# Mish part of a fused attention and MLP kernel: token tiles of 512 columns in place of 384

## The chip, the cores and the metric

The kernel runs on one core of a Trainium2 chip. The metric is the device time of one execution, in microseconds (us). The profile counts the core's span from the first to the last instruction, and names the engines: PE is TensorE's matmul stream and PEld its weight loads, DVE is VectorE, ACT is ScalarE, POOL is GpSimd, SP is SyncE, which issues the transfers.

## The reference, cut to what matters

Three layers follow each other: a landmark attention (4 batches of 576 tokens, 8 heads of 64), a gated MLP, and a Mish MLP. The change lies in the last one alone. Its input x has 2304 tokens (4 times 576) by 512.

```python
def _moe2_ref(x, w_in, w_out):          # 2304 x 512, 512 x 2048, 2048 x 512
    h = x @ w_in
    sp = np.where(h > 20.0, h, np.log1p(np.exp(np.minimum(h, 20.0))))
    g = h * np.tanh(sp)
    return (g @ w_out).astype(np.float32)
```

## The kernel before

Attention and the gated MLP are issued as steps in an order that a table (`ORDER`, line 24) writes out; each step is for one engine and each engine works its steps in that order. At its end the step list leaves `Y[b]` (512 features by 576 tokens for each batch, in SBUF). Behind it stands the Mish part, lines 1047 to 1131, as plain loops. Only the part behind the table, and the four steps `yh`/`yl` of the table that split the first tile's activations (`add_ys`, line 1029), depend on the tile width `TT`.

Every product of the Mish part keeps fp32 accuracy by splitting both operands in a high part (`fp32r`) and the rest: `mm3` (line 188) makes three matmuls, high times high (L189), high times rest (L190), rest times high (L191). Each of them has its own weight load of 128 by 128.

The part works on 6 tiles of `TT` = 384 tokens, and in each on 16 blocks `f` of 128 hidden features: 96 iterations `n`. One call `p2(n)` (line 1107) issues for one iteration:

- `z_mm(n)`, the first product: 4 blocks `k` of 128 input features, `mm3` each, so 12 matmuls. The stationary operand is a block of w_in, the moving one the split activations `ys(t, k, hl)`, 384 columns wide. The result is bank `n % 4` of PSUM (`bank[0:4]`, printed as ps_83 to ps_86).
- `o_mm(n - 3)`, the second product of the iteration three before: for each of the tile's 3 blocks `c` of 128 tokens one `mm3`, so 9 matmuls. Stationary are the split Mish values `gb(n, hl)`, moving is a block of w_out, 512 columns wide. They add up over the 16 blocks `f` in one accumulator bank per `c`, and three of the four banks `bank[4:8]` (ps_87 to ps_90) are in use in a tile; the next tile starts one bank further (`(3 * t + c) % 4`). After the last `f`, ACT (c = 0, 2) and DVE (c = 1) copy the accumulators to `osb`, and SP issues a store for each.
- `tick(n)` (line 1101): ACT takes Mish of the bank twice, into `emx` in fp32 (L1103) and into `gb(n, 0)` in fp32r (L1104); DVE subtracts the two into `gb(n, 1)` (L1105). Both `gb` and `emx` have three places, used in turn (`n % 3`).
- for `n` under 12, the remaining weights: one block of w_in or w_out is split by ACT and POOL, and a later one is loaded by SP and decoded by DVE and ACT.
- `split_y` for the next tile, on ACT (high part) and DVE (rest), one `k` in each of four iterations.

Since `z_mm(n)` stands ahead of `o_mm(n - 3)` on PE, ACT and DVE have the stretch of some two iterations to bring `gb(n)`, before PE wants it. In the first three iterations there is no second product, and in the last three calls no first one. `gb(n, 0)` may only be written when `o_mm(n - 3)` has read the same place.

Of the kernel before, what the change touches and what calls it, by code (L numbers as in the profile page):

```python
# [7 lines left out]
F32 = mybir.dt.float32  # L8
F32R = mybir.dt.float32r
# [3 lines left out]
ACTF = mybir.ActivationFunctionType  # L13
# [138 lines left out]
def kernel(  # L152
# [14 lines left out]
    nc = tc.nc  # L167
    V, G, S, T = nc.vector, nc.gpsimd, nc.scalar, nc.tensor
    B, S_LEN = v.shape[0], v.shape[1]
# [1 line left out]
    NP = H // 2  # L171
    BLK_T = S_LEN // L
    HALF = S_LEN // 2
    TT = 384
    NS = w1.shape[1] // 128
    scale = 1.0 / float(D) ** 0.5

    def f32(ap):
        return ap.bitcast(F32)
# [8 lines left out]
    def mm3(o, lh, ll, rh, rl, first, last):  # L188
        T.matmul(out=o, lhsT=lh, rhs=rh, start=first, stop=False)  # L189
        T.matmul(out=o, lhsT=lh, rhs=rl, start=False, stop=False)  # L190
        T.matmul(out=o, lhsT=ll, rhs=rh, start=False, stop=last)  # L191
# [5 lines left out]
    def top_bits(e, w):  # L197
        q = w.bitcast(U16)
        if e == "ACT":

            S.activation(w[..., 0], q[..., 1], ACTF.Copy, scale=2.0 ** -13, bias=2.0 ** -14 - 0.5)  # L201
        else:
            V.tensor_scalar(q[..., 0], q[..., 1], 13, None, op0=ALU.logical_shift_right)

    def sign(w):
        q = w.bitcast(U16)
        V.tensor_scalar(q[..., 1], q[..., 3], 0x8000, None, op0=ALU.bitwise_and)  # L207

    def rescale(w):
        S.activation(f32(w[..., 1]), f32(w[..., 1]), ACTF.Copy, scale=2.0 ** -112)  # L210
# [5 lines left out]
    def copy(e, o, x):  # L216
        if e == "ACT":
            S.activation(o, x, ACTF.Copy)  # L218
        else:
            (G if e == "POOL" else V).tensor_scalar(o, x, 1.0, 0.0, op0=ALU.mult, op1=ALU.add)  # L220

    def less(e, o, x, hi):
        (G if e == "POOL" else V).tensor_tensor(o, x, f32(hi), op=ALU.subtract)
# [6 lines left out]
    def kept(tag, shape, dtype, name):  # L230

        return pe.tile(shape, dtype, tag=tag, name=name)
# [4 lines left out]
    Y = {}  # L237
# [10 lines left out]
    RAW = kept("RAW", [128, 4, 512, 2], I32, "raw")  # L248
    LATE = {}
    bank = [ps.tile([128, 512], F32, name=f"ps{i}") for i in range(8)]  # L250
# [12 lines left out]
    def step(name, eng, after, fn, take=(), free=()):  # L263
        for key in free:
            users.setdefault(key, set()).add(name)
        steps[name] = ((eng,) if isinstance(eng, str) else eng,
                       [a for a in dict.fromkeys(after) if a in steps], fn, dict(take), tuple(free))
# [6 lines left out]
    def got(key):  # L274
        pool, i = at[key]
        return pools[pool][i]
# [620 lines left out]
    HS = []  # L897

    def swap(e):
        attn_pool.close()  # L900
        pw = ctx.enter_context(tc.tile_pool(name="pw", bufs=1, reuse_waits="tile"))
        HS.extend(pw.tile([128, 8 * 2 * HALF], F32R, name=f"hs{i}") for i in range(2))
        HS.append(pw.tile([128, 4, 1024], F32R, name="wx"))
        HS.append(pw.tile([128, TT], F32R, name="gx"))
        HS.append(pw.tile([128, 3, TT], F32, name="emx"))

    def hs(u):
        return HS[got(f"hs {u}")].rearrange("p (k h s) -> p k h s", k=8, h=2)
# [29 lines left out]
    NF = wi2.shape[1] // 512  # L938
    wq = [(k, j, i) for j in range(NF) for k in (0, 1) for i in range(4)]

    def late(tag, shape, dtype, name):
        if name not in LATE:
            LATE[name] = kept(tag, shape, dtype, name)
        return LATE[name]

    def wpart(n, i):

        if n < 4:
            x = HS[2][:, n]
        elif n < 7:  # L950
            x = M[n - 4]
        elif n < 11:
            x = late(f"W{(n - 7) // 2}", [128, 2, 1024], F32R, f"wxw{(n - 7) // 2}")[:, (n - 7) % 2]
        elif n == 11:
            x = late("A", [128, 1024], F32R, "wxa")
        elif n < 20:
            x = late(f"H{(n - 12) // 2}", [128, 2, 1024], F32R, f"wx{(n - 12) // 2}")[:, n % 2]
        elif n < 28:
            x = W3[(n - 20) // 4][:, 2 * (n % 4):2 * (n % 4) + 2].rearrange("p a n -> p (a n)")
        else:  # L960
            x = HS[got("hs 7")][:, (n - 28) * 1024:(n - 27) * 1024]
        return x[:, i * 512:(i + 1) * 512]
# [7 lines left out]
    def w_load(n, r):  # L970
        k, j, i = wq[n]
        src = wi2[i * 128:(i + 1) * 128, j * 512:(j + 1) * 512] if k == 0 else wo2[(4 * j + i) * 128:(4 * j + i + 1) * 128, :]
        nc.sync.dma_start(out=r, in_=words(src))

    def w_raw(n):
        n = EARLY + (n - EARLY) % RAW6 if n >= EARLY else n
        if n >= EARLY + 4:
            return late("LT", [128, 2, 512, 2], I32, "wl")[:, n - EARLY - 4]
        return got(f"x{n}")
# [46 lines left out]
    def ys0(k, hl):  # L1026
        return HS[got("ys")][:, (2 * k + hl) * TT:(2 * k + hl + 1) * TT]

    def add_ys(k):
        step(f"yh {k}", "ACT", ["sh 7 0", f"ye 0 {k}", f"ye 1 {k}"] + [f"yh {i}" for i in range(k)],  # L1030
             lambda e: copy(e, ys0(k, 0), Y[0][:, k, 0:TT]), {} if k else {"ys": "hs"})
        step(f"yl {k}", "DVE", [f"yh {k}"], lambda e: less(e, ys0(k, 1), Y[0][:, k, 0:TT], ys0(k, 0)))

# [11 lines left out]


    NT = out.shape[0]
    NTILE = NT // TT
    E = HS[4]
    R = HS[got("ys")].rearrange("p (r s) -> p r s", r=12)  # L1050
    GX = [HS[3], HS[got("hs 7")][:, 4096:4096 + TT]]

    def ys(t, k, hl):
        return (late("RAW", [128, 8, TT], F32R, "ys") if t % 2 else R)[:, 2 * k + hl, :]

    def split_y(t, k):
        done = 0
        while done < TT:
            b, s = divmod(t * TT + done, S_LEN)
            w = min(TT - done, S_LEN - s)  # L1060
            o = slice(done, done + w)
            copy("ACT", ys(t, k, 0)[:, o], Y[b][:, k, s:s + w])
            less("DVE", ys(t, k, 1)[:, o], Y[b][:, k, s:s + w], ys(t, k, 0)[:, o])
            done += w

    def gb(n, hl):
        return GX[hl] if n % 3 == 2 else R[:, 8 + 2 * (n % 3) + hl, :]

    NFC = 4 * NF
    NN = NTILE * NFC  # L1070
    zt, ot, oc = {}, {}, [0]

    def z_mm(n):
        t, f = divmod(n, NFC)
        c = slice((f % 4) * 128, (f % 4 + 1) * 128)
        p = zt[n] = bank[n % 4][:, 0:TT]
        for k in range(4):
            u = 8 * (f // 4) + k
            mm3(p, wpart(u, 0)[:, c], wpart(u, 1)[:, c], ys(t, k, 0), ys(t, k, 1), k == 0, k == 3)

    def o_mm(n):
        t, f = divmod(n, NFC)
        u = 8 * (f // 4) + 4 + f % 4
        for c in range(3):
            if f == 0:
                ot[c] = bank[4 + (3 * t + c) % 4]
            s = slice(c * 128, (c + 1) * 128)
            mm3(ot[c], gb(n, 0)[:, s], gb(n, 1)[:, s], wpart(u, 0), wpart(u, 1), f == 0, f == NFC - 1)
        if f == NFC - 1:
            osb = late("LT", [128, 4, 512], F32, "osb")  # L1090
            for c in range(3):
                o = osb[:, oc[0] % 4]
                oc[0] += 1
                if c % 2 == 0:
                    S.activation(o, ot[c], ACTF.Copy)
                else:
                    V.tensor_copy(o, ot[c])
                r0 = t * TT + c * 128
                nc.sync.dma_start(out=out[r0:r0 + 128, :], in_=o)

    def tick(n):
        x = E[:, n % 3, :]
        S.activation(x, zt[n], ACTF.Mish)  # L1103
        S.activation(gb(n, 0), zt.pop(n), ACTF.Mish)  # L1104
        V.tensor_tensor(gb(n, 1), x, f32(gb(n, 0)), op=ALU.subtract)  # L1105

    def p2(n):
        if n < NN:
            z_mm(n)
        if n >= 3:  # L1110
            o_mm(n - 3)
        if n < NN:
            tick(n)
        u = EARLY + n
        if u < len(wq):
            copy("ACT", wpart(u, 0), f32(w_raw(u)[..., 0]))
            less("POOL", wpart(u, 1), f32(w_raw(u)[..., 0]), wpart(u, 0))
            if u + RAW6 < len(wq):
                w_load(u + RAW6, w_raw(u))
            if n >= 2 and u - 2 + RAW6 < len(wq):  # L1120
                r = w_raw(u - 2 + RAW6)
                top_bits("DVE", r)
                sign(r)
                rescale(r)
                join(r)
        split_at = (12, 13, 14, 15) if n < NFC else (4, 7, 10, 13)
        if n % NFC in split_at and n + NFC < NN:
            split_y(n // NFC + 1, split_at.index(n % NFC))

    for n in range(NN + 3):  # L1130
        p2(n)


# [38 lines left out]
```

## Time and profile before

| | us |
|---|---|
| median of 3 runs (lowest to highest) | 787.62 (783.45 to 1238.11) |
| the profiled execution's own time | 785.8 |
| its span | 784.0 |
| PE busy in the span | 758.1 |
| ACT busy / DVE busy in the span | 343.7 / 348.6 |
| first matmul of the Mish part starts at | 378.19 |
| last matmul of the Mish part starts at | 779.74 |

The times of the rows are counted from the span's start; the profiled execution's own time has 1.8 us more than its span. A matmul's row gives its start and how long it was under way; matmuls overlap, so the pace of PE is read from the distance of two starts, here called a step. The duration of a row is longer than a step.

### The profile page before, as it was taken

How to read it: one execution, taken by the hardware profiler on the slowest of the kernel's cores; microseconds unless marked ns; L12 is line 12 of the kernel's file. 1: busy time of each engine (PE TensorE's matmuls, PEld its weight loads, DVE VectorE, ACT ScalarE, POOL GpSimd, SP SyncE). 2: the span in 40 equal slices, each digit the busy share in tenths (PEclk: the TensorE clock that was granted, in tenths of full speed). 3: DMA queues.
4: the chain of work that ended last, by engine and by line, in shares of the span. 5: the costliest groups of instructions: out<-in, count | busy, mean ns of one | idle time of the engine just before them, and what ended most of it. 6: DMA issues, size and time to landing. Idle time of an engine off the chain costs nothing.

```text
span 784.0 us, 13585 instructions
## 1 busy us (share of the span) xinstructions
PE 758.1 (97%) x5380; PEld 650.6 (83%) x5380; DVE 348.6 (44%) x719; ACT 343.7 (44%) x772; POOL 119.2 (15%) x120
## 2 busy tenths in 40 slices
PE   6887999999999999999999999999999999999998
PEld 2644457888799889999998998999999999899896
DVE  5878867887875663755271221121111112111111
ACT  5456465666653664876444222232222222222221
POOL 0427100520153213331232000000000000000000
PEclk8989899999999999999999999999999999999999
DMA  8993255742431314343220010010010001001001
GB/s 311 376 320 97 82 188 161 253 129 82 135 109 56 107 55 135 109 135 108 81 82 0 1 41 1 0 41 1 1 40 2 1 1 41 0 1 41 1 0 41
DMA packets 38384, 65.96 MB, mean 84 GB/s; under 512 B 3888, under 2 KB 20400, under 8 KB 38320
## 3 DMA queue, kind: packets, MB, share of 16 engines
q1 hardware_dynamic: 38320, 65.09, 24.9%
q8 instruction: 42, 0.69, 0.4%
q14 instruction: 22, 0.18, 0.1%
HBM read 60.36 MB, written 4.72 MB: 83 GB/s over the span
## 4 chain that ended last, share of the span: by engine, by line
PE 90%; DVE 5%; DMA 2%; issue 1%; ACT 1%; SPq 1%; POOL 0%; DVEq 0%; ACTq 0%; POOLq 0%
PE ps L189 26%; PE ps L191 26%; PE ps L190 25%; PE ps L356 6%; PE ps L850 2%; DVE raw L207 2%; PE ps L450 2%; DMA raw<-in_wo_dram 1%; DVE raw L214 1%; DMA raw<-in_w_dram 1%; PE ps L528 1%; PE ps L646 1%; PE ps L587 1%; PE ps L566 0%; PE ps L506 0%
## 5 line engine op out<-in xcount | busy, mean ns | idle before, releaser
L1105 DVE TENSOR_TENSOR hs<-emx,hs 128x384 fp32r<-128x384 f32 x64 | 35.7, 559 | 202.1 <-ACT hs L1104 201.9
L1103 ACT ACTIVATE emx<-ps 128x384 f32<-128x384 f32 x96 | 47.1, 490 | 130.3 <-PE ps L191 130.3
L189 PE MATMUL ps<-hs,W 128*128 128x288 f32 (+1 forms) x304 | 91.8, 302 | 0.0
L190 PE MATMUL ps<-hs,W 128*128 128x288 f32 (+1 forms) x304 | 91.4, 301 | 0.0
L191 PE MATMUL ps<-hs,W 128*128 128x288 f32 (+1 forms) x304 | 91.4, 301 | 0.0
L207 DVE TENSOR_SCALAR raw<-raw 128x512 uint16<-128x512 uint16 x84 | 72.7, 894 | 37.7 <-ACT raw L201 37.3
L189 PE MATMUL ps<-AT,M 128*128 128x288 f32 x256 | 78.2, 305 | 0.1
L191 PE MATMUL ps<-AT,M 128*128 128x288 f32 x256 | 75.5, 295 | 0.0
L190 PE MATMUL ps<-AT,M 128*128 128x288 f32 x256 | 75.5, 295 | 0.0
L356 PE MATMUL ps<-wo,raw 128*128 128x512 f32 x128 | 62.9, 651 | 7.2 <-DVE raw L214 7.2
L210 ACT ACTIVATE raw<-raw 128x512 f32<-128x512 f32 x84 | 55.8, 678 | 28.7 <-DVE raw L207 24.6
L201 ACT ACTIVATE raw<-raw 128x512 int32<-128x512 uint16 x79 | 52.6, 672 | 29.1 <-DMA raw<-in_w_dram 14.3
L1104 ACT ACTIVATE hs<-ps 128x384 fp32r<-128x384 f32 x64 | 31.5, 492 | 76.0 <-PE ps L190 76.0
L1105 DVE TENSOR_TENSOR hs<-emx,gx 128x384 fp32r<-128x384 f32 x32 | 17.9, 558 | 99.9 <-ACT gx L1104 99.7
L356 PEld LDWEIGHTS ps<-wo,raw 128*128 128x128 f32 x128 | 27.0, 215 | 40.3 <-issue 29.1
L190 PEld LDWEIGHTS ps<-hs,W 128*128 128x128 f32 x304 | 57.4, 189 | 0.5
L189 PEld LDWEIGHTS ps<-hs,W 128*128 128x128 f32 x304 | 57.0, 187 | 1.0 <-ACT y L218 0.4
L191 PEld LDWEIGHTS ps<-hs,W 128*128 128x128 f32 x304 | 57.3, 189 | 0.0
L189 PEld LDWEIGHTS ps<-AT,M 128*128 128x128 f32 x256 | 48.0, 188 | 7.2 <-issue 2.1
L191 PEld LDWEIGHTS ps<-AT,M 128*128 128x128 f32 x256 | 48.1, 188 | 0.0
L190 PEld LDWEIGHTS ps<-AT,M 128*128 128x128 f32 x256 | 48.1, 188 | 0.0
L218 ACT ACTIVATE a<-ps 128x288 f32<-128x288 f32 x64 | 26.1, 410 | 36.0 <-PE ps L191 35.6
(217 smaller groups left out, 1712.9 us busy)
## 6 DMA issues: line engine op xcount, KB each, us to landing
raw<-in_w_dram SPq DMA_DIRECT2D x128, 128.0 KB, 2.6
raw<-in_wo_dram SPq DMA_DIRECT2D x22, 512.0 KB, 4.6
raw<-in_w3T_dram SPq DMA_DIRECT2D x32, 256.0 KB, 6.9
raw<-in_wi_dram SPq DMA_DIRECT2D x14, 512.0 KB, 4.2
k<-in_kT_dram SPq DMA_DIRECT2D x8, 576.0 KB, 8.1
q<-in_qT_dram SPq DMA_DIRECT2D x8, 576.0 KB, 8.6
out_dram<-osb SPq DMA_DIRECT2D x18, 256.0 KB, 2.1
vt<-in_v_dram SPq DMA_DIRECT2D x4, 1024.0 KB, 8.3
```

Source lines behind the costliest of these rows:

```text
L189: T.matmul(out=o, lhsT=lh, rhs=rh, start=first, stop=False)
L190: T.matmul(out=o, lhsT=lh, rhs=rl, start=False, stop=False)
L191: T.matmul(out=o, lhsT=ll, rhs=rh, start=False, stop=last)
L201: S.activation(w[..., 0], q[..., 1], ACTF.Copy, scale=2.0 ** -13, bias=2.0 ** -14 - 0.5)
L207: V.tensor_scalar(q[..., 1], q[..., 3], 0x8000, None, op0=ALU.bitwise_and)
L210: S.activation(f32(w[..., 1]), f32(w[..., 1]), ACTF.Copy, scale=2.0 ** -112)
L218: S.activation(o, x, ACTF.Copy)
L356: T.matmul(out=got(f"acc{i}"), lhsT=f32(got(f"w3{n}")[:, o:o + 128, 0]), rhs=WO0[j // 4][:, j % 4], start=j == 0, stop=j == 7)
L450: T.matmul(out=sc[0:w, i, p * 64:p * 64 + 64], lhsT=st["q"][:, p, t0:t0 + w], rhs=bdk[:, p, :], start=True, stop=True)
L1103: S.activation(x, zt[n], ACTF.Mish)
L1104: S.activation(gb(n, 0), zt.pop(n), ACTF.Mish)
L1105: V.tensor_tensor(gb(n, 1), x, f32(gb(n, 0)), op=ALU.subtract)
```

## The change

The tile width becomes 512, and the tiles are listed with their width, four of 512 tokens and a last one of 256. So there are 80 iterations. In a tile of 512, `z_mm` has 12 matmuls of 512 columns and `o_mm` 12 (four blocks `c`); in the last tile 12 of 256 columns and 6. The second product follows two iterations behind (`o_mm(n - 2)`), `gb` has two places and `emx` one. The accumulators are `bank[4 + c]` in each tile, and the copies out go to ACT for even `c` and to DVE for odd `c`.

```diff
-    TT = 384
+    TT = 512
...
-        HS.append(pw.tile([128, TT], F32R, name="gx"))
-        HS.append(pw.tile([128, 3, TT], F32, name="emx"))
+        HS.append(pw.tile([128, 2, TT], F32R, name="gx"))
+        HS.append(pw.tile([128, TT], F32, name="emx"))
...
-    NTILE = NT // TT
+    tiles = [(t0, min(TT, NT - t0)) for t0 in range(0, NT, TT)]
     E = HS[4]
-    R = HS[got("ys")].rearrange("p (r s) -> p r s", r=12)
-    GX = [HS[3], HS[got("hs 7")][:, 4096:4096 + TT]]
+    R = HS[got("ys")][:, 0:8 * TT].rearrange("p (r s) -> p r s", r=8)
+    GX = [HS[3][:, 0], HS[3][:, 1], HS[got("ys")][:, 8 * TT:9 * TT], HS[got("hs 7")][:, 4096:4096 + TT]]
...
     def gb(n, hl):
-        return GX[hl] if n % 3 == 2 else R[:, 8 + 2 * (n % 3) + hl, :]
+        return GX[2 * (n % 2) + hl][:, 0:tiles[n // NFC][1]]
...
-        p = zt[n] = bank[n % 4][:, 0:TT]
+        p = zt[n] = bank[n % 4][:, 0:tiles[t][1]]
...
-        for c in range(3):
-            if f == 0:
-                ot[c] = bank[4 + (3 * t + c) % 4]
+        for c in range(w // 128):
             s = slice(c * 128, (c + 1) * 128)
-            mm3(ot[c], gb(n, 0)[:, s], gb(n, 1)[:, s], wpart(u, 0), wpart(u, 1), f == 0, f == NFC - 1)
+            mm3(bank[4 + c], gb(n, 0)[:, s], gb(n, 1)[:, s], wpart(u, 0), wpart(u, 1), f == 0, f == NFC - 1)
...
-        x = E[:, n % 3, :]
+        x = E[:, 0:tiles[n // NFC][1]]
...
-        if n >= 3:
-            o_mm(n - 3)
+        if n >= 2:
+            o_mm(n - 2)
...
-    for n in range(NN + 3):
+    for n in range(NN + 2):
```

`split_y` cuts a tile where a batch ends, as before, but by the tile's own width: the pieces of the second tile are 64 and 448 columns in place of 192 and 192.

On PE, at the first second product, the order before is this (M_1032 is a block of w_out, wx and wxw are blocks of w_in, hs_2358 holds the split activations and before also `gb`):

```order
L189 MATMUL ps_88<-M_1032,hs_2358 128x512
L190 MATMUL ps_88<-M_1032,hs_2358 128x512
L191 MATMUL ps_88<-M_1032,hs_2358 128x512
L189 MATMUL ps_89<-M_1032,hs_2358 128x512
L190 MATMUL ps_89<-M_1032,hs_2358 128x512
L191 MATMUL ps_89<-M_1032,hs_2358 128x512
L189 MATMUL ps_83<-hs_2358,wxw_3263 128x384
L190 MATMUL ps_83<-hs_2358,wxw_3263 128x384
L191 MATMUL ps_83<-hs_2358,wxw_3263 128x384
```

and of the changed kernel:

```order
L189 MATMUL ps_88<-M_1032,gx 128x512
L190 MATMUL ps_88<-M_1032,gx 128x512
L191 MATMUL ps_88<-M_1032,gx 128x512
L189 MATMUL ps_89<-M_1032,gx 128x512
L190 MATMUL ps_89<-M_1032,gx 128x512
L191 MATMUL ps_89<-M_1032,gx 128x512
L189 MATMUL ps_90<-M_1032,gx 128x512
L190 MATMUL ps_90<-M_1032,gx 128x512
L191 MATMUL ps_90<-M_1032,gx 128x512
L189 MATMUL ps_86<-hs_2358,wx 128x512
L190 MATMUL ps_86<-hs_2358,wx 128x512
```

Three accumulators with a 384-wide first product behind them become four with a 512-wide one, and the width of the moving operand no longer changes between the two products.

On PE, in the last tile, before (the last matmuls of the first product with the last block of w_in, and the second product behind it):

```order
L189 MATMUL ps_86<-ys,W_66 128x384
L190 MATMUL ps_86<-ys,W_66 128x384
L191 MATMUL ps_86<-ys,W_66 128x384
L189 MATMUL ps_90<-hs_2359,gx 128x512
L190 MATMUL ps_90<-hs_2359,gx 128x512
L191 MATMUL ps_90<-hs_2359 128x512
L189 MATMUL ps_87<-hs_2359,gx 128x512
L190 MATMUL ps_87<-hs_2359,gx 128x512
L191 MATMUL ps_87<-hs_2359 128x512
L189 MATMUL ps_88<-hs_2359,gx 128x512
L190 MATMUL ps_88<-hs_2359,gx 128x512
L191 MATMUL ps_88<-hs_2359 128x512
```

and now:

```order
L189 MATMUL ps_86<-hs_2358,W_66 128x256
L190 MATMUL ps_86<-hs_2358,W_66 128x256
L191 MATMUL ps_86<-hs_2358,W_66 128x256
L189 MATMUL ps_87<-hs_2359,hs_2358 128x512
L190 MATMUL ps_87<-hs_2359,hs_2358 128x512
L191 MATMUL ps_87<-hs_2359 128x512
L189 MATMUL ps_88<-hs_2359,hs_2358 128x512
L190 MATMUL ps_88<-hs_2359,hs_2358 128x512
L191 MATMUL ps_88<-hs_2359 128x512
L189 MATMUL ps_87<-hs_2359,gx 128x512
```

The first product is 256 wide there, and one second product has six matmuls in place of nine.

On DVE, where the first tile's accumulators are copied out, before:

```order
L223 TENSOR_TENSOR ys<-y_2581,ys 128x192
L223 TENSOR_TENSOR ys<-y_3391,ys 128x192
L1105 TENSOR_TENSOR hs_2358<-emx,hs_2358 128x384
L1105 TENSOR_TENSOR hs_2359<-emx,gx 128x384
L1097 COPY osb<-ps_88 128x512
L1105 TENSOR_TENSOR hs_2358<-emx,hs_2358 128x384 x2
L1105 TENSOR_TENSOR hs_2359<-emx,gx 128x384
```

and now:

```order
L223 TENSOR_TENSOR ys<-y_2581,ys 128x64
L223 TENSOR_TENSOR ys<-y_3391,ys 128x448
L1103 TENSOR_TENSOR gx<-emx,gx 128x512
L1096 COPY osb<-ps_88 128x512
L1096 COPY osb<-ps_90 128x512
L1103 TENSOR_TENSOR hs_2359<-emx,hs_2358 128x512
L1103 TENSOR_TENSOR gx<-emx,gx 128x512
```

DVE has two accumulators to copy in place of one at the end of a wide tile, and the subtraction of the next Mish values stands behind both.

## Rows read from the trace of the kernel before

**Rows 1.** The page: busy time by engine, the TensorE clock by slice, the chain by engine.
```profile
PE 758.1 (97%) x5380; PEld 650.6 (83%) x5380; DVE 348.6 (44%) x719; ACT 343.7 (44%) x772; POOL 119.2 (15%) x120
...
PEclk8989899999999999999999999999999999999999
...
PE 90%; DVE 5%; DMA 2%; issue 1%; ACT 1%; SPq 1%; POOL 0%; DVEq 0%; ACTq 0%; POOLq 0%
```

**Rows 2.** Windows: length; busy us (x) of PE, PEld, DVE, ACT, POOL; clock, DMA, GB/s.
```profile
378.19:779.97 401.78, 401.78 (x2018) 363.93 (x2016) 84.41 (x148) 119.62 (x251) 17.29 (x12) 1.00 0.05 18
391.12:730.29 339.17, 339.17 (x1702) 307.26 (x1702) 73.10 (x129) 100.41 (x214) 13.20 (x9) 1.00 0.05 17
```

**Rows 3.** Timeline of PE in the steady state: start us, us, engine line op.
```profile
499.64 0.39 PE L189 MATMUL ps<-W,hs 128*128 128x512 f32 x1
...
501.72 0.33 PE L189 MATMUL ps<-ys,W 128*128 128x384 f32 x1
...
503.82 0.39 PE L189 MATMUL ps<-hs,hs 128*128 128x512 f32 x1
```

**Rows 4.** Timeline of PE from the product before through the start of the Mish part.
```profile
375.02 0.30 PE L189 MATMUL ps<-hs,W 128*128 128x288 f32 x1
...
378.19 0.34 PE L189 MATMUL ps<-hs,wx 128*128 128x384 f32 x1
...
380.30 0.33 PE L189 MATMUL ps<-hs,wx 128*128 128x384 f32 x1
...
386.54 0.39 PE L189 MATMUL ps<-M,hs 128*128 128x512 f32 x1
```

**Rows 5.** Timeline of PE in the last second products.
```profile
773.85 0.39 PE L189 MATMUL ps<-hs,hs 128*128 128x512 f32 x1
...
777.93 0.39 PE L189 MATMUL ps<-hs,gx 128*128 128x512 f32 x1
...
779.74 0.39 PE L191 MATMUL ps<-hs 128*128 128x512 f32 x1
```

**Rows 6.** Groups by form from 360 us: busy, mean ns, idle before.
```profile
L1103 ACT ACTIVATE emx<-ps 128x384 f32<-128x384 f32 x96 | 47.1, 490 | 130.3 <-PE ps L191 130.3
...
L1105 DVE TENSOR_TENSOR hs<-emx,hs 128x384 fp32r<-128x384 f32 x64 | 35.7, 559 | 202.1 <-ACT hs L1104 201.9
...
L1095 ACT ACTIVATE osb<-ps 128x512 f32<-128x512 f32 x12 | 7.2, 599 | 21.5 <-PE ps L191 21.5
...
L1097 DVE COPY osb<-ps 128x512 f32<-128x512 f32 x6 | 4.2, 692 | 17.5 <-PE ps L191 17.5
...
L223 DVE TENSOR_TENSOR ys<-y,ys 128x192 fp32r<-128x192 f32 x8 | 2.5, 351 | 0.0
...
L189 PEld LDWEIGHTS ps<-hs,W 128*128 128x128 f32 x46 | 8.6, 187 | 0.0
```

**Rows 7.** Timeline of ACT and DVE in the same iteration as rows 3.
```profile
501.75 0.49 ACT L1104 ACTIVATE hs<-ps 128x384 fp32r<-128x384 f32 x1 [1.42 <-PE ps L190]
...
502.27 0.56 DVE L1105 TENSOR_TENSOR hs<-emx,hs 128x384 fp32r<-128x384 f32 x1 [3.16 <-ACT hs L1104]
```

**Rows 8.** Timeline of DVE in the first iterations.
```profile
390.39 0.56 DVE L1105 TENSOR_TENSOR hs<-emx,hs 128x384 fp32r<-128x384 f32 x1
...
394.73 0.56 DVE L1105 TENSOR_TENSOR hs<-emx,hs 128x384 fp32r<-128x384 f32 x1
```

**Rows 9.** Timeline at the first change of tile: DVE, then PE.
```profile
439.89 0.62 DVE L223 TENSOR_TENSOR ys<-y,ys 128x192 fp32r<-128x192 f32 x2
...
440.62 0.38 PE L190 MATMUL ps<-ys,wx 128*128 128x384 f32 x1
...
440.85 0.34 PE L191 MATMUL ps<-ys,wx 128*128 128x384 f32 x1
```

**Rows 10.** Timeline of ACT: first split of activations, and the last copy out.
```profile
363.39 1.75 ACT L218 ACTIVATE hs<-y 128x384 fp32r<-128x384 f32 x4
...
780.17 0.60 ACT L1095 ACTIVATE osb<-ps 128x512 f32<-128x512 f32 x1 [0.76 <-PE ps L191]
```

More of the change, by code (lines that the diff above doesn't have):

```diff
@@ L1047 @@
     NT = out.shape[0]
-    NTILE = NT // TT
+    tiles = [(t0, min(TT, NT - t0)) for t0 in range(0, NT, TT)]
     E = HS[4]
-    R = HS[got("ys")].rearrange("p (r s) -> p r s", r=12)
-    GX = [HS[3], HS[got("hs 7")][:, 4096:4096 + TT]]
+    R = HS[got("ys")][:, 0:8 * TT].rearrange("p (r s) -> p r s", r=8)
+    GX = [HS[3][:, 0], HS[3][:, 1], HS[got("ys")][:, 8 * TT:9 * TT], HS[got("hs 7")][:, 4096:4096 + TT]]
     def ys(t, k, hl):
-        return (late("RAW", [128, 8, TT], F32R, "ys") if t % 2 else R)[:, 2 * k + hl, :]
+        return (late("RAW", [128, 8, TT], F32R, "ys") if t % 2 else R)[:, 2 * k + hl, 0:tiles[t][1]]
     def split_y(t, k):
+        t0, w = tiles[t]
         done = 0
[L1058 to L1064, printed above, removed]
+        while done < w:
+            b, s = divmod(t0 + done, S_LEN)
+            n = min(w - done, S_LEN - s)
+            o = slice(done, done + n)
+            copy("ACT", ys(t, k, 0)[:, o], Y[b][:, k, s:s + n])
+            less("DVE", ys(t, k, 1)[:, o], Y[b][:, k, s:s + n], ys(t, k, 0)[:, o])
+            done += n
+    NFC = 4 * NF
+    NN = len(tiles) * NFC
+    zt, ot, oc = {}, {}, [0]
     def gb(n, hl):
-        return GX[hl] if n % 3 == 2 else R[:, 8 + 2 * (n % 3) + hl, :]
-    NFC = 4 * NF
-    NN = NTILE * NFC
-    zt, ot, oc = {}, {}, [0]
+        return GX[2 * (n % 2) + hl][:, 0:tiles[n // NFC][1]]
     def z_mm(n):
@@ L1082, in o_mm @@
         t, f = divmod(n, NFC)
+        t0, w = tiles[t]
         u = 8 * (f // 4) + 4 + f % 4
-        for c in range(3):
-            if f == 0:
-                ot[c] = bank[4 + (3 * t + c) % 4]
+        for c in range(w // 128):
             s = slice(c * 128, (c + 1) * 128)
-            mm3(ot[c], gb(n, 0)[:, s], gb(n, 1)[:, s], wpart(u, 0), wpart(u, 1), f == 0, f == NFC - 1)
+            mm3(bank[4 + c], gb(n, 0)[:, s], gb(n, 1)[:, s], wpart(u, 0), wpart(u, 1), f == 0, f == NFC - 1)
         if f == NFC - 1:
             osb = late("LT", [128, 4, 512], F32, "osb")
-            for c in range(3):
-                o = osb[:, oc[0] % 4]
-                oc[0] += 1
+            for c in range(w // 128):
+                o = osb[:, c]
                 if c % 2 == 0:
-                    S.activation(o, ot[c], ACTF.Copy)
+                    S.activation(o, bank[4 + c], ACTF.Copy)
                 else:
-                    V.tensor_copy(o, ot[c])
-                r0 = t * TT + c * 128
-                nc.sync.dma_start(out=out[r0:r0 + 128, :], in_=o)
+                    V.tensor_copy(o, bank[4 + c])
+                nc.sync.dma_start(out=out[t0 + c * 128:t0 + (c + 1) * 128, :], in_=o)
     def tick(n):
-        x = E[:, n % 3, :]
+        x = E[:, 0:tiles[n // NFC][1]]
         S.activation(x, zt[n], ACTF.Mish)
```

## The prediction

> **What bounds the kernel now.** I read the page first. PE is busy in 97% of the span, its clock is at the full level of 2.4 GHz in nearly every slice, and 90% of the chain that ended last is PE's [rows 1]. Then the windows: the Mish part is 401.78 us, half of the span, and PE is busy in all of it at the full clock, while DVE has 84 us and ACT 120 us of work [rows 2]. So only what changes PE's own pace, or makes PE wait, can move the time. The pace comes from the timeline. In the steady state nine matmuls of the second product take 501.72 - 499.64 = 2.08 us, a step of 231.2 ns, and twelve of the first take 503.82 - 501.72 = 2.10 us, 175.3 ns [rows 3]. The window from 391.12 to 730.29 holds 1702 matmuls, so 81 iterations of 21 in 339.17 us, 4.187 us each [rows 2]: the pattern of rows 3 repeats without a gap.
>
> Two places show a faster step. The first products of iterations 1 to 3, which stand behind one another with no second product between them, take (386.54 - 380.30)/36 = 173.3 ns a step; that of iteration 0, behind 288-wide matmuls, took 2.11 us for twelve, 175.8 ns [rows 4]. The 18 matmuls of the second product that follow one another at the end take (777.93 - 773.85)/18 = 226.7 ns [rows 5]. So where the width of the moving operand stays the same the step is shorter, and where it has just changed it is longer: 0.026 us a first product and 0.041 us a second one. ACT and DVE work during the fast stretches too, so their traffic is not the likely reason. The 288-wide product before has (378.19 - 375.02)/24 = 132.1 ns [rows 4]. From 132.1 over 173.3 to 226.7 the step grows by 0.42 to 0.43 ns a column; what is left over at zero columns, some 10 to 13 ns, is paid for every matmul whatever its width.
>
> **The change part by part.** The columns streamed stay the same, 96 x (12 x 384 + 9 x 512) = 884,736 before and after. The number of matmuls falls from 2016 to 64 x 24 + 16 x 18 = 1824: the first product has 192 fewer, the second still 864.
>
> The sum for PE, by the steps without a change of width for the four wide tiles, where every moving operand is now 512 wide: 64 x 24 x 226.7 ns = 348.2 us. In the last tile the widths alternate (256 and 512), so I take the longer second-product step: 16 x 6 x 231.2 ns = 22.2 us. A 256-wide step is not in the trace. The line from 288 and 384 gives 118 ns, that from 384 and 512 gives 120; I take 119.5, and as bounds 115.5 (173.3 x 256/384) and 132.1, the row next to it. 192 x 119.5 = 22.9 us, and 16 x 0.026 = 0.4 us for the changes of width. Together 393.7 us against 401.8, so **8.1 us less**. The other end for the 512-wide step is the 231.2 ns that the second product has now [rows 3]: then the wide tiles take 355.1 us and the gain is 1.2 us. I take 226.7 because the same pattern, the same operands and the same engine gave it as soon as the widths stopped changing.
>
> On the weight loads a record and a rule differ. A load is recorded with 187 ns, and this while the 288-wide steps were 132 ns [rows 4, 6], so the records overlap and do not set the pace there. The Trainium skill ("TensorE: Matmul & The Clock Gate", LDWEIGHTS) has a load of 128 columns at P / 1.2, about 107 ns. By that rule the 256-wide step of 119.5 ns still covers the load, and the 22.9 us stay; if a load really held the array for the recorded time they would be 36.1 us. No row here shows a mean step under 130 ns with such loads, so the point is open; it is the third rival.
>
> Work off PE. A Mish of 384 columns is 490 ns; of 512 I take the 600 ns of ACT's 512-wide copy, and at most 490 x 512/384 = 653. A subtraction is 559 ns; from the 351 ns at 192 columns, 1.04 ns a column, 512 come to 0.69 us, as DVE's 512-wide copy has it; at most 745 [rows 6]. ACT and DVE keep two thirds of their time free [rows 2], so the amounts cost nothing under PE's steps.
>
> The shorter pipeline. Today ACT's second Mish waits until the second product that reads the old place is nearly through; it starts 0.03 us after the next first product does, and the subtraction follows 0.52 us later [rows 3, 7]. Afterwards the same wait exists: after `z_mm(n)` comes `o_mm(n - 2)`, 12 x 226.7 = 2.7 us, then Mish 0.6 and the subtraction 0.7, so `gb(n)` is there about 4.1 us behind the end of `z_mm(n)`. PE wants it after four products, 10.9 us. Slack 6.8 us; in the last tile 1.39 + 0.03 + 0.9 = 2.3 us against 5.6. Behind the waiting Mish on ACT stand only splits for the next tile and weights. The single `emx`: the next Mish may start when the subtraction is over, 4.1 us against a period of 5.4, so nothing is late. If this cover were gone, each wait would stand on PE; the second rival from below prices one.
>
> The first iterations: DVE, with decoding and the waits on ACT, needs 394.73 - 390.39 = 4.34 us an iteration [rows 8], slightly more than PE's 4.19, and lags. With 0.13 us more for the subtraction (0.19 at most) it is about 4.5 us against PE's 5.44, so the lag shrinks. The first split in the table grows from 1.75 to about 2.3 us on ACT [rows 10], thirteen microseconds ahead of its first use: nothing.
>
> The change of tile. The last matmul but one of the first product at the first change ran 0.23 us instead of 0.17, since DVE was still splitting (0.05 us lost) [rows 9]. With wider splits DVE ends some 0.4 us later, but PE comes to that place 0.5 us later too; bounds 0 and 0.3 us, I take 0. The accumulators: PE wants bank 4 first, 2.7 us after the last second product of a tile; its copy can begin 2 us before that end and is 0.6 us. The fourth is DVE's second copy, about 0.8 us after the end, wanted 4.8 us after it. Nothing; if the copies came late by one copy in each change, 4 x 0.6 = 2.4 us. At the very end DVE copies last (0.69 us) and not ACT (0.60) [rows 6, 10]: 0.1 us more.
>
> Sum: 785.8 - 8.1 + 0.1 = **778 us**, against the profiled execution's own time. The median shown is 787.62, the lowest run 783.45; the profiled one lies between them, so runs differ by about 2 us on either side.
>
> **The rivals.**
> 1. The longer step stays although the widths are equal, because it belongs to the alternation of the two products (other stationary and moving tensors), not to the width. For it: a constant 288-wide stream is not even from matmul to matmul. Against it: the first product of iteration 0 was slow behind 288-wide matmuls with no second product near [rows 4]. Then the gain is 1.2 us: 784.7. The Trainium skill (same page, Back-to-back issue gap) gives N/2.4 + 2.5 ns, a fixed part of 2.5 ns; by it 192 fewer matmuls give 0.5 us and the time would be 785.3, beside this rival. The trace disagrees with its level: 173.3 ns at 384 columns, where the rule gives 162.5.
> 2. PE waits for `gb` in the shorter pipeline. For it: two places in place of three, one `emx`, and DVE slower than PE in the first iterations [rows 8]. Against it: 6.8 us of slack. If the twelve iterations that still decode weights lost 0.5 us each, the time would be 784.
> 3. The slow side: the 256-wide step is held by the weight load at its recorded 187 ns. Place: the 192 matmuls of the last tile's first product; price 192 x (187 - 119.5) = 13.0 us; it decides as soon as the step exceeds 119.5 + 8.0/0.192 = 161 ns. Then 791. Against it: 132.1 ns steps with the same loads.
>
> **How the numbers follow.** My forecast 55%, rival 1 27%, rival 2 6%, rival 3 7%, and 5% for what I don't see. The forecast's own range is 775.5 to 780.5 from the 2 us of the runs; rivals 1 and 2 with the same 2 us reach to 787, and I end at 788. Below, 774. Rival 3 is left out. 2% of the time, about what a measurement of this kernel can tell from no change, is 15.8 us: no case reaches it, faster needs an unseen gain of twice the size (2%), slower rival 3 or 2 at more than their price (3%).
>
> **What would show it.** Right: in the wide tiles twelve matmuls in 2.72 us for both products, an iteration in 5.44 us; the Mish part in about 394 us; the last tile 2.85 us an iteration; no idle PE at the changes of tile. Rival 1 shows as 2.77 us for twelve; rival 2 as idle PE ahead of L189 or L191 with DVE or ACT as releaser; rival 3 as 2.2 us for the 256-wide first product. If PE's stretch is as long as said but the time is not, the end or the part ahead of 378 us has moved, and the argument from PE alone is wrong.

## The result

| | before | changed |
|---|---|---|
| median of 6 runs, us | 784.33 | 776.23 |
| lowest to highest, us | 783.28 to 1238.11 | 774.72 to 777.21 |
| ratio, with its 95% interval | | 0.9892 (0.9868 to 0.9916) |
| profiled execution: own time / span, us | 785.8 / 784.0 | 776.88 / 775.1 |
| Mish part, first matmul's start to last one's start, us | 401.55 | 393.06 |

The changed kernel is 8.1 us faster by the medians, 1.1%: a gain that lies clear of 1 by its interval and inside the 2% that the prediction called no change. By the ratio, which leaves the one slow execution of 1238.11 us out, it is 8.5 us. The forecast was 778 us, by a gain of 8 us.

The page of the changed kernel, with the same lines as [rows 1], shows the same picture as before: PE is busy in 97% of the span, its granted clock is at the full level in nearly every slice, and PE has 91% of the chain that ended last.

```profile
PE 750.3 (97%) x5188; PEld 616.3 (80%) x5188; DVE 350.4 (45%) x706; ACT 337.6 (44%) x737; POOL 120.1 (15%) x120
...
PEclk9989899999999999999999999999999999999999
...
PE 91%; DVE 5%; DMA 2%; issue 1%; ACT 1%; POOL 0%; SPq 0%; DVEq 0%; POOLq 0%
```

So it is the pace of PE that differs. The windows of the Mish part, with the columns of [rows 2], are the whole part and the stretch from iteration 3's first product to the last tile's first matmul:

```profile
377.77:771.06 393.29, 393.29 (x1826) 329.40 (x1824) 83.69 (x134) 113.30 (x217) 18.50 (x12) 1.00 0.06 19
388.66:720.49 331.83, 331.83 (x1465) 275.03 (x1464) 73.50 (x113) 93.38 (x173) 15.89 (x10) 1.00 0.05 17
```

PE is busy in all of both, at a granted clock of 1.00. The second holds 61 iterations in 331.83 us, 5.440 us each; with 24 matmuls that is 226.7 ns a step. The timeline of PE in one of them, first products at 589.94 and 595.38, a second product at 592.66, answers to [rows 3]:

```profile
589.94 0.39 PE L189 MATMUL ps<-hs,wx 128*128 128x512 f32 x1
...
592.66 0.39 PE L189 MATMUL ps<-wx,gx 128*128 128x512 f32 x1
...
595.38 0.39 PE L189 MATMUL ps<-hs,wx 128*128 128x512 f32 x1
```

Both products take 2.72 us for their twelve matmuls, the step that [rows 5] showed at the end alone. At the start of the part, answering to [rows 4]:

```profile
377.77 0.39 PE L189 MATMUL ps<-hs,wx 128*128 128x512 f32 x1
...
383.22 0.39 PE L189 MATMUL ps<-hs,wx 128*128 128x512 f32 x1
...
385.94 0.39 PE L189 MATMUL ps<-M,gx 128*128 128x512 f32 x1
```

From 383.22 to 385.94 the third first product takes 2.72 us, as long as one behind a second product; before, these two differed. In the last tile the first product is 256 wide (740.14), the second 512 (741.57):

```profile
740.14 0.28 PE L189 MATMUL ps<-hs,wxw 128*128 128x256 f32 x1
...
741.57 0.40 PE L189 MATMUL ps<-wx,gx 128*128 128x512 f32 x1
...
742.96 0.28 PE L189 MATMUL ps<-hs,wxw 128*128 128x256 f32 x1
```

The first takes 1.43 us, 119.4 ns a step, the second 1.39 us, 231 ns: there the widths alternate, and the second product has the slower step that all of them had before.

Off PE, the groups by form answer to [rows 6]: Mish and subtraction at 512 columns, mean 597 and 693 ns.

```profile
L1101 ACT ACTIVATE emx<-ps 128x512 f32<-128x512 f32 x64 | 38.2, 597 | 112.9 <-PE ps L191 112.9
...
L1103 DVE TENSOR_TENSOR gx<-emx,gx 128x512 fp32r<-128x512 f32 x32 | 22.2, 693 | 140.4 <-ACT gx L1102 140.4
```

The change of the first tile, as [rows 9]: the last two steps of the first product and the next second product stand 0.23 us apart, so the 0.05 us lost before is gone.

```profile
461.64 0.39 PE L190 MATMUL ps<-ys,wx 128*128 128x512 f32 x1
...
461.87 0.39 PE L191 MATMUL ps<-ys,wx 128*128 128x512 f32 x1
...
462.10 0.39 PE L189 MATMUL ps<-hs,gx 128*128 128x512 f32 x1
```

DVE in the first iterations, as [rows 8]: one subtraction to the next is 5.44 us, PE's own period, and the idle time ahead of each (1.02 us in brackets) shows that DVE now has time left.

```profile
394.70 0.69 DVE L1103 TENSOR_TENSOR hs<-emx,hs 128x512 fp32r<-128x512 f32 x1 [1.02 <-ACT hs L1102]
...
400.14 0.69 DVE L1103 TENSOR_TENSOR gx<-emx,gx 128x512 fp32r<-128x512 f32 x1 [1.02 <-ACT gx L1102]
```

### The profile page after: what moved, and what is told of

It is laid out like the page before. It is cut to its first block, busy times and chain, and to the rows that moved or that the text cites. A ratio compares the mean times of both kernels' runs of the same rounds, so it can differ in the third digit from the quotient of the medians.

```text
span 775.1 us, 13036 instructions
## 1 busy us (share of the span) xinstructions
PE 750.3 (97%) x5188; PEld 616.3 (80%) x5188; DVE 350.4 (45%) x706; ACT 337.6 (44%) x737; POOL 120.1 (15%) x120
## 4 chain that ended last, share of the span: by engine, by line
PE 91%; DVE 5%; DMA 2%; issue 1%; ACT 1%; POOL 0%; SPq 0%; DVEq 0%; POOLq 0%
PE ps L189 26%; PE ps L191 26%; PE ps L190 26%; PE ps L356 6%; PE ps L850 2%; PE ps L450 1%; DVE raw L207 1%; DMA raw<-in_wo_dram 1%; PE ps L646 1%; DVE raw L214 1%; PE ps L528 1%; PE ps L587 1%; DMA k<-in_kT_dram 1%; PE ps L566 1%; PE ps L506 0%
## 5 line engine op out<-in xcount | busy, mean ns | idle before, releaser
L1101 ACT ACTIVATE emx<-ps 128x512 f32<-128x512 f32 (+1 forms) x80 | 44.3, 554 | 131.6 <-PE ps L191 131.6
L1103 DVE TENSOR_TENSOR gx<-emx,gx 128x512 fp32r<-128x512 f32 (+1 forms) x40 | 25.6, 639 | 158.6 <-ACT gx L1102 158.6
L189 PE MATMUL ps<-hs,W 128*128 128x288 f32 (+2 forms) x304 | 92.7, 305 | 0.0
L190 PE MATMUL ps<-hs,W 128*128 128x288 f32 (+2 forms) x304 | 92.4, 304 | 0.0
L191 PE MATMUL ps<-hs,W 128*128 128x288 f32 (+2 forms) x304 | 92.2, 303 | 0.0
L207 DVE TENSOR_SCALAR raw<-raw 128x512 uint16<-128x512 uint16 x84 | 74.4, 917 | 37.6 <-ACT raw L201 37.2
L1103 DVE TENSOR_TENSOR hs<-emx,hs 128x512 fp32r<-128x512 f32 (+1 forms) x40 | 25.6, 639 | 136.6 <-ACT hs L1102 136.6
L189 PE MATMUL ps<-AT,M 128*128 128x288 f32 x256 | 78.3, 306 | 1.0 <-DVE M L223 0.9
L191 PE MATMUL ps<-AT,M 128*128 128x288 f32 x256 | 75.5, 295 | 0.0
L210 ACT ACTIVATE raw<-raw 128x512 f32<-128x512 f32 x84 | 55.8, 678 | 29.8 <-DVE raw L207 25.6
L189 PEld LDWEIGHTS ps<-hs,W 128*128 128x128 f32 x304 | 57.1, 188 | 1.8 <-ACT y L218 0.4
L191 PEld LDWEIGHTS ps<-hs,W 128*128 128x128 f32 x304 | 57.5, 189 | 1.2
L189 PEld LDWEIGHTS ps<-AT,M 128*128 128x128 f32 x256 | 48.1, 188 | 8.2 <-issue 2.1
L1102 ACT ACTIVATE gx<-ps 128x512 fp32r<-128x512 f32 (+1 forms) x40 | 22.2, 556 | 61.2 <-PE ps L190 61.2
L191 PEld LDWEIGHTS ps<-AT,M 128*128 128x128 f32 x256 | 48.1, 188 | 0.0
L1102 ACT ACTIVATE hs<-ps 128x512 fp32r<-128x512 f32 (+1 forms) x40 | 22.3, 557 | 54.7 <-PE ps L190 54.7
```

## The experiments

Each theory speaks of the step of PE. Theory W: a matmul is slower just behind a change of the moving operand's width. Rival P: the new places of `gb` and `emx`, the shorter pipeline or the fixed banks made the steps faster. Rival A: the alternation of two products with different tensors makes them slow, whatever the width.

**e1: the shorter pipeline, fewer places and fixed banks alone.** The kernel before with 384-wide tiles and this edit (cut):

```diff
-        return GX[hl] if n % 3 == 2 else R[:, 8 + 2 * (n % 3) + hl, :]
+        return R[:, 8 + 2 * (n % 2) + hl, :]
...
-                ot[c] = bank[4 + (3 * t + c) % 4]
+                ot[c] = bank[4 + c]
...
-        x = E[:, n % 3, :]
+        x = E[:, 0, :]
...
-        if n >= 3:
-            o_mm(n - 3)
+        if n >= 2:
+            o_mm(n - 2)
```

> The kernel before with its tiles of 384, but the second product two iterations behind, two places for the split Mish values, one for the fp32 Mish, and each accumulator always in the same bank. Theory W (a matmul is slower just behind a change of the moving operand's width): nothing changes, first product 2.106 us, second 2.081 us an iteration, ratio to the kernel before 1.000 (0.998 to 1.002). Rival P (the new places, the shorter pipeline or the fixed banks bring the faster steps): second product near 2.040 us and first near 2.080 us, 6 us less, ratio 0.992. If the shorter pipeline costs waits: above 1.002 with idle PE ahead of L189 or L191.

Measured: ratio 1.0007 (0.9987 to 1.0027). The timeline of PE in an iteration, first product, second product, next first product:

```profile
543.06 0.33 PE L189 MATMUL ps<-hs,wx 128*128 128x384 f32 x1
...
545.17 0.39 PE L189 MATMUL ps<-wx,hs 128*128 128x512 f32 x1
...
547.25 0.33 PE L189 MATMUL ps<-hs,wx 128*128 128x384 f32 x1
```

2.11 and 2.08 us; [rows 3] have 2.10 and 2.08. So the shorter pipeline, two places in place of three, one `emx` and the fixed banks bring nothing, and with 384-wide tiles they cost nothing either: PE has no wait in the part, although DVE needed 4.3 us an iteration at its start and PE 4.19:

```profile
392.96 0.56 DVE L1105 TENSOR_TENSOR hs<-emx,hs 128x384 fp32r<-128x384 f32 x1
...
397.28 0.56 DVE L1105 TENSOR_TENSOR hs<-emx,hs 128x384 fp32r<-128x384 f32 x1
```

The two places of e1 lie where `gb` lay before; the changed kernel's new ones are tested by e3, which has them and the slow steps too. With both, rival P falls.

**e5: the same work, half the changes of width.** The kernel before, with the products issued in pairs:

```diff
-        if n < NN:
-            z_mm(n)
-        if n >= 3:
-            o_mm(n - 3)
+        if n % 2 == 0:
+            for i in (n, n + 1):
+                if i < NN:
+                    z_mm(i)
+            for i in (n - 3, n - 2):
+                if 0 <= i < NN:
+                    o_mm(i)
```

> The kernel before with its tiles of 384 and all of its work, but the products issued in pairs: two first products, then two second ones. The number of matmuls is the same, the number of changes of width is halved. Theory W: the excess of 0.026 us stands at every other first product alone, that of 0.041 us at every other second product, or over both where it goes on past nine matmuls: 48 x 0.026 = 1.2 us to 48 x 0.067 = 3.2 us less, ratio 0.996 to 0.9985. Rival P (places, depth, banks): no change, ratio 1.000. If a matmul were slower for what it reads or writes and not for what ran before it: no change either.

Measured: ratio 0.9945 (0.9928 to 0.9963), and in the trace a Mish part of 398.51 us in place of 401.55. The timeline of one pair of each (two first products, two second ones, the next first one):

```profile
538.08 0.33 PE L189 MATMUL ps<-hs,wx 128*128 128x384 f32 x1
...
540.18 0.34 PE L189 MATMUL ps<-hs,wx 128*128 128x384 f32 x1
...
542.26 0.39 PE L189 MATMUL ps<-wx,hs 128*128 128x512 f32 x1
...
544.34 0.39 PE L189 MATMUL ps<-wx,gx 128*128 128x512 f32 x1
...
546.38 0.33 PE L189 MATMUL ps<-hs,wx 128*128 128x384 f32 x1
```

The two first products take 2.10 and 2.08 us, the two second ones 2.08 and 2.04 us: only the leading one of each pair, which stands just behind a change, has the excess. 3.0 us are the upper end of what was expected; 48 x (0.026 + 0.041) is 3.2. The whole ratio is larger (4.3 us), but the part of the program ahead of the Mish part, which is unchanged, ended at 378.05 us in this profile and between 375.67 and 379.79 in others, so only the 3.0 us are put down to the edit; they lie within the ratio's interval, 2.9 to 5.7 us. Pairs halve the alternation of the two products as well as the changes of width, so e5 does not tell theory W from rival A.

**e2 and e3: the width of the second product.** Both leave out a quarter of the output's columns, and the copies and stores are narrowed with them. In the kernel before (e2) and in the changed one (e3, `bank[4 + c]` for `ot[c]`), cut to the product:

```diff
-            mm3(ot[c], gb(n, 0)[:, s], gb(n, 1)[:, s], wpart(u, 0), wpart(u, 1), f == 0, f == NFC - 1)
+            mm3(ot[c][:, 0:384], gb(n, 0)[:, s], gb(n, 1)[:, s], wpart(u, 0)[:, 0:384], wpart(u, 1)[:, 0:384], f == 0, f == NFC - 1)
```

> The kernel before, with the second product 384 columns wide in place of 512: a quarter of the output's columns is left out, and its copies and stores are narrower. Both products then have moving operands of 384 columns. Theory W: every step 173.3 ns, first product 2.080 us, second 9 x 173.3 = 1.560 us, an iteration 3.64 us, the Mish part about 349.5 us. Rival A (the slow steps belong to the alternation of the two products, with their different tensors, not to the width): the first product stays at 2.106 us and the second has about 0.03 us over 1.560.

Measured: one execution, Mish part 349.44 us (expected 349.5). The timeline of PE in an iteration:

```profile
520.75 0.33 PE L189 MATMUL ps<-hs,wx 128*128 128x384 f32 x1
...
522.83 0.33 PE L189 MATMUL ps<-wx,hs 128*128 128x384 f32 x1
...
524.39 0.33 PE L189 MATMUL ps<-hs,wx 128*128 128x384 f32 x1
```

The first product takes 2.08 us behind a second one, the second 1.56 us behind a first one: the mean step is 173.3 ns in both. The tensors still alternate, the widths do not; rival A falls for 384 columns. For 512 the changed kernel itself shows it, with all of its work: its two products alternate as well, at 226.7 ns a step.

> The changed kernel, with the second product 384 columns wide in place of 512: a quarter of the output's columns is left out. In the wide tiles the first product is now 512 and the second 384 wide, so the widths alternate again. Theory W: the 512-wide first product starts with slower steps, 229 to 236 ns, 0.04 to 0.055 us over 12 x 226.7 = 2.720 us, and the 384-wide second product has 0.026 us over 12 x 173.3 = 2.080 us, in its first six steps. Rival A or P: both flat, 2.720 and 2.080 us.

Measured, in one execution, a first product from its start, its tenth matmul, the second product, and the next first one:

```profile
569.63 0.39 PE L189 MATMUL ps<-hs,wx 128*128 128x512 f32 x1
...
571.71 0.39 PE L189 MATMUL ps<-hs,wx 128*128 128x512 f32 x1
...
572.39 0.33 PE L189 MATMUL ps<-wx,gx 128*128 128x384 f32 x1
...
574.50 0.39 PE L189 MATMUL ps<-hs,wx 128*128 128x512 f32 x1
```

Nine steps of 231.1 ns (571.71 - 569.63), then three of 226.7, and 2.11 us for the 384-wide second product. In ns the steps of the first product read 229, 233, 237, 223, 231, 236, 229, 232, 230, 227, 227, 226, those of the second 171, 175, 179, 185, 175, 181 and then 173 or 174. So the changed kernel gets the slow steps back when its widths alternate, with the roles of the products exchanged: the pattern belongs to the pair of widths. After 512 to 384 it lasts six matmuls, after 384 to 512 nine, which is just all of a second product before.

**e6: the fixed part of a matmul.** The changed kernel, all of its work done, each 512-wide matmul as two of 256:

```diff
-        for k in range(4):
-            u = 8 * (f // 4) + k
-            mm3(p, wpart(u, 0)[:, c], wpart(u, 1)[:, c], ys(t, k, 0), ys(t, k, 1), k == 0, k == 3)
+        for x in range(0, tiles[t][1], 256):
+            h = slice(x, x + 256)
+            for k in range(4):
+                u = 8 * (f // 4) + k
+                mm3(p[:, h], wpart(u, 0)[:, c], wpart(u, 1)[:, c], ys(t, k, 0)[:, h], ys(t, k, 1)[:, h], k == 0, k == 3)
...
-            mm3(bank[4 + c], gb(n, 0)[:, s], gb(n, 1)[:, s], wpart(u, 0), wpart(u, 1), f == 0, f == NFC - 1)
+            for h in (slice(0, 256), slice(256, 512)):
+                mm3(bank[4 + c][:, h], gb(n, 0)[:, s], gb(n, 1)[:, s], wpart(u, 0)[:, h], wpart(u, 1)[:, h], f == 0 and h.start == 0, f == NFC - 1 and h.start == 256)
```

> The changed kernel with all of its work, but every 512-wide matmul of the Mish part cut into two of 256 columns, each with its own weight load: 3456 matmuls of one width in place of 1824. If each matmul has a fixed part of about 13 ns over its columns, and a constant width gives an even stream: every step 119.5 to 120 ns, the Mish part 3456 x 119.8 = 414 us, 21 us more than the 393 us of the changed kernel, the time 797 to 799 us, ratio to the kernel before 1.015 to 1.02. If the fixed part were 2.5 ns: 378 us, ratio 0.97. If the recorded 188 ns of a weight load held the array: 650 us, ratio 1.3.

Measured: 799.21 us, ratio 1.0196 (1.0177 to 1.0215). First matmul, one iteration, last matmul:

```profile
376.94 0.28 PE L189 MATMUL ps<-hs,wx 128*128 128x256 f32 x1
...
602.60 0.28 PE L189 MATMUL ps<-hs,wx 128*128 128x256 f32 x1
...
605.48 0.28 PE L189 MATMUL ps<-wx,gx 128*128 128x256 f32 x1
...
608.36 0.28 PE L189 MATMUL ps<-hs,wx 128*128 128x256 f32 x1
...
792.56 0.28 PE L191 MATMUL ps<-hs 128*128 128x256 f32 x1
```

24 matmuls take 2.88 us, 120.0 ns each, in both products. The part is 415.6 us from start to start; 3456 x 120.0 = 414.7, and 1.0 us was lost around one wait at the first change of tile, where the first half now wants all split activations in half the time:

```profile
465.46 0.38 PE L190 MATMUL ps<-ys,wx 128*128 128x256 f32 x1 [0.40 <-DVE ys L223]
```

120.0 and 226.7 ns at 256 and 512 columns give 0.417 ns a column, one column in a period of 2.4 GHz, and 13.3 ns fixed. The weight loads are recorded with 192 ns each in this run, longer than a step, so this duration does not set the pace.

**e4 and e7: the pipeline with short iterations.** e4 is the changed kernel with `TT = 256`; e7 in addition has three places for `gb` and `emx` and a second product three iterations behind, as the kernel before.

> The changed kernel with tiles of 256 in place of 512, all work done: nine tiles, 144 iterations of twelve 256-wide and six 512-wide matmuls. By the steps of the changed kernel's last tile an iteration is 1.433 + 1.387 = 2.82 us, the Mish part 406 us if PE never waits, the time 789 us. But the weights still to be decoded in the first twelve iterations keep DVE 4.3 us an iteration, and the pipeline is two deep: theory with waits: PE waits there some 1.5 us an iteration for ten iterations, 15 us, the Mish part about 420 us, the time near 803 us, with DVE as the releaser ahead of L191. If the two places alone were too few, waits would show in later tiles too.

Measured: 791.8 us, ratio 1.0101 (1.0076 to 1.0127), Mish part 410.68 us. Where PE waited, by the list of waits (engine, line, whom it waited for: us in total, times, longest):

```profile
PE ps L189 <- ACT gx L1102: 1.8, 2, 0.9
...
PE ps L189 <- ACT hs L1102: 1.7, 2, 0.9
```

The timeline of PE at the first of the four shows a second product that starts 1.06 us behind the matmul ahead of it, 0.78 us of which PE is idle for ACT:

```profile
393.97 0.28 PE L191 MATMUL ps<-hs,wxa 128*128 128x256 f32 x1
...
395.03 0.50 PE L189 MATMUL ps<-wx,hs 128*128 128x512 f32 x1 [0.78 <-ACT hs L1102]
```

So a two-deep pipeline can be too short, as rival 2 of the prediction had it, but in four iterations (7 to 10), not ten, and with ACT's second Mish ahead of L189 as the releaser, not DVE ahead of L191. Behind ACT stands DVE's decoding all the same:

```profile
397.81 0.65 ACT L210 ACTIVATE raw<-raw 128x512 f32<-128x512 f32 x1 [2.27 <-DVE raw L207]
...
402.65 0.38 ACT L1102 ACTIVATE hs<-ps 128x256 fp32r<-128x256 f32 x1
...
406.69 0.38 ACT L1102 ACTIVATE gx<-ps 128x256 fp32r<-128x256 f32 x1
...
407.96 0.38 ACT L1102 ACTIVATE hs<-ps 128x256 fp32r<-128x256 f32 x1
```

ACT's share of the decoding (L210) is issued ahead of Mish and waited 2.27 us for DVE, and so one second Mish follows the other after 4.04 us, against PE's 2.82; with no L210 ahead of it the next one follows after 1.27 us, and the waits end. With the steps behind each wait 4.7 us were lost, a third of what I expected; that the two iterations in hand took up the lag of the first ones is the likely reason. Later tiles have no waits.

> The tiles of 256 again, all work done, but the second product three iterations behind, three places for the split Mish values and for the fp32 Mish, as the kernel before has them. With two places PE waited for ACT's second Mish in four iterations, 4.7 us in all in the Mish part of 410.7 us. If the depth of the pipeline is what decides there, one more iteration of 2.82 us in hand takes that much off the first wait and the total: 1.9 us of waits are left, the Mish part about 408 us. If the waits came from the decoding alone and the depth did not matter, 4.7 us stay and the part is 410.7 us again.

Measured: 795.29 us, ratio 1.0129 (1.0053 to 1.0204), Mish part 409.87 us. The same list:

```profile
PE ps L189 <- ACT gx L1102: 1.8, 2, 0.9
...
PE ps L189 <- ACT hs L1102: 0.9, 1, 0.9
```

The waits fall, but the part is only 0.8 us shorter, in place of 2.8. My price was wrong: by the order of issue, one more iteration of depth puts one first product more ahead of the second (12 x 120 ns = 1.44 us), not a whole iteration. The lag was 0.6 us larger in this run: ACT's second Mish of iteration 8, which releases the last of the waits in both runs, started 31.64 us behind the part's first matmul in place of 31.02. 1.44 - 0.6 is the 0.8 us.

## Why the prediction was right

**PE alone sets the end.** This held: the part fell from 401.55 to 393.06 us, 8.5 us, of the 8.9 us between the two profiled executions; the rest, 0.4 us, lies ahead of the part, which began at 377.77 in place of 378.19 us. That was not forecast and is chance as far as these runs tell: the start of the part lies between 375.67 and 379.79 us in them. So it is the length of the part, not the total, that tests the sum. The end is as long as before: 775.1 - 770.83 us by the last row, 4.27, as 784.0 - 779.74.

```profile
770.83 0.39 PE L191 MATMUL ps<-hs 128*128 128x512 f32 x1
```

So the 0.1 us that I added for DVE's later copy is not to be seen in the end, although that copy is over 1.11 us behind the last matmul's start, ACT's before 1.03 us [rows 5, 10]:

```profile
771.25 0.69 DVE L1096 COPY osb<-ps 128x512 f32<-128x512 f32 x1 [2.10 <-PE ps L191]
```

**The even step of 226.7 ns for the wide tiles** was read from 18 matmuls and carried most of the sum: 348.2 us said, 64 x 5.440 = 348.2 by the 61 iterations measured. e1 shows that the pipeline is not the reason, e2 and the changed kernel itself that equal widths are enough while the products alternate, e3 that unequal ones bring the slow steps back. Rival 1 would have had 231 ns.

**The 256-wide step** of 119.5 ns, drawn between two lines, came as 119.4 behind a second product and 120.0 in an even stream. Rival 3, a load that holds the array for the 187 ns of its record, is excluded by these steps. The fixed part was put at 10 to 13 ns; it is 13.3 at 256, 384 and 512 columns. (The two lines through the rows of before give 8.5 and 13 ns.) The Trainium skill ("TensorE: Matmul & The Clock Gate", Back-to-back issue gap) has N/2.4 + 2.5 ns, for what it calls the isolated gap of a single matmul; e6's 0.417 ns a column agrees with its N/2.4, but for this stream of fp32r matmuls, each with its own load, no run shows its 2.5 ns.

**The changes of width in the last tile** were taken as 0.026 us for each first product. That term was wrong in sign, with little weight: behind 512 columns the twelve 256-wide matmuls take 1.433 us, in an even stream 1.440. The 16 first products took 22.9 us, and the 0.4 us on top of it did not come. The 0.027 us of each second product was right. With this 0.4 us, the 0.1 us at the end and the 0.4 us ahead of the part, 777.8 becomes the 776.9 measured.

**How the 8.5 us divide.** With even steps the part would be 96 x (12 x 173.3 + 9 x 226.7) ns = 395.5 us before and 348.2 + 192 x 120.0 + 96 x 226.7 ns = 393.0 us afterwards: 2.5 us from fewer matmuls (192 x 13.3 ns). The other 6 us were the slow steps behind changes of width; 6.3 us of them stood in the part before, and 0.3 us are left, nearly all in the last tile.

**What was priced at nothing** was nothing: `gb` with two places, one `emx`, the four accumulators, the changes of tile. PE has no wait in the part. Iteration 3's subtraction, the row at 394.70, ends 4.0 us behind the end of its first product (388.66 + 2.72), where 4.1 us were forecast and 10.9 allowed. Rival 2 needed iterations of 2.8 us to appear (e4); with 5.44 us the first iterations even have time left. The slope used for the subtraction was misread: (559 - 351)/192 is 1.08 ns a column and not 1.04. It makes 698 ns in place of 690, measured 693, and no term of the sum hangs on it.

Left open: why a change of width slows the next matmuls at all, and why the size depends on the pair (288 to 384 costs 0.030 us, 288 to 512 0.005). Equal widths are not always an even stream either: the 288-wide matmuls ahead of the part step by 129 to 136 ns, in a pattern that repeats with every twelve, and no run here tells why. Three places with tiles of 512 and a last tile in pairs of products were not tried; at 0.3 us the latter is below what these runs can tell.

## What to carry to other kernels

On a kernel that PE bounds, read the step from the starts of neighbouring matmuls, in several places: a stretch that runs faster than the same instructions elsewhere shows what can be had. Here each matmul with its own weight load paid 13.3 ns over its columns, and two interleaved products with moving widths of 384 and 512 paid 26 and 41 ns at each change, so the tile size that gives both the same, widest moving operand was worth more by the equal widths (6.0 us) than by the matmuls it saves (2.5 us). The shorter pipeline was free with iterations of 5.44 us, and also with 4.19 us where DVE needed 4.3 in the first ones (e1); it cost 4.7 us where PE's iteration was 2.82 us and ACT, held by DVE's decoding, needed 4.04 (e4). So compare PE's iteration with that of the slowest engine behind it, and count for how many iterations it lags.

## What was not expected

The slow steps have the same pattern in every iteration, within 2 ns, and end after a fixed number of matmuls: six after 512 to 384, nine after 384 to 512, five after 256 to 512. And a change can also be a gain: the first step after 512 to 256 is 113 ns in place of 120, and in e3's last tile twelve matmuls of 256 columns behind 384 take 1.426 us in place of 1.440. So "slower behind a change of width" holds for 384 and 512 columns in either direction and is no rule for all pairs.
